# K and q turned on VectorE instead of TensorE, for nine of twelve chunks of a fused attention and MLP kernel

## Chip, cores and metric

One NeuronCore of a Trainium2 chip runs the whole program. The metric is the device time of one execution in microseconds (us); the kernel before takes 1048.77 us, the median of 3 runs (1047.95 to 1049.24).

## Reference

Three layers follow each other. The first is a linear attention with a delta rule: for each of 4 x 8 batch-heads, a 48 x 48 state is read by the query and updated by the key, over 768 positions. The other two are MLPs on 3072 tokens (384 to 2048 to 384), with different activations.

```python
k_n = k / (np.linalg.norm(k, axis=-1, keepdims=True) + 1e-06)
for t in range(S):
    y[:, :, t] = einsum('bhd,bhde->bhe', q[:, :, t], state)
    v_old = einsum('bhde,bhd->bhe', state, kt)
    state = state + bt * einsum('bhd,bhe->bhde', kt, vt - v_old)
# then, on x = y as 3072 tokens x 384:
h = x @ w_in;  x = where(h >= 1, h, where(h <= -1, 0, (h + 1) ** 2 / 4)) @ w_out
h = x @ w_in2; out = (h * clip(h + 3, 0, 6) / 6) @ w_out2
```

## The kernel before

**Attention by chunks.** The 768 positions are cut into 12 chunks (0 to 11) of 64. The 32 batch-heads are 16 units of two heads; a unit's two heads lie in the two halves of the partitions. For a chunk, `front` loads K in natural layout (`KN`), forms norms, brings K and q into transposed layout (`KTT` and `QQ`, head dimension on the partitions, both inside the tile `KQ`; two sets, for even and odd chunks), multiplies them (`products`), and inverts a triangular matrix (`inverse`, most of it as a row of GpSimd steps, L630 and L635, from the transposed matrix that VectorE writes at L688). `chain` then applies the state, forms the update and the output; the output is put into `XB`, 16 rows of each head by a detour over `YS` and a DMA.

**K and q before the change.** For each half `hb` of the batch-heads, `load_tok` (L434) loads K and q with positions on the partitions, two DMAs each of 96 KB in pieces of 192 bytes, into one of two staging buffers `ST`; `transposes` (L516) turns them by four TensorE transposes of 128 columns (L523) into one PSUM bank, and one copy of 112 x 512 out of it follows, on ScalarE or VectorE (L385 or L387); for K a further copy of 112 x 128 repeats a part of it shifted. A chunk has so four groups of four transposes, eight DMAs and four evacuations, and two of the small copies.

**MLP.** Layer 1 runs over seven blocks of tokens: chunk 0, chunk 1, then pairs of chunks. A block goes through 16 slices `f` of the hidden dimension: nine matmuls into a PSUM bank (`H`), an elementwise path (ScalarE L976 and L977, VectorE L978, a copy by L385 into `GH`, VectorE L374 into `GL`), and nine matmuls from `GH` and `GL` (`O`). `O` of a slice is issued after `H` of the next. A finished block leaves by six DMAs (`X<-XB`, L1028). Layer 2 runs over six blocks in the same manner; its weights are loaded into `KQ` once attention has finished with it.

**What sets the order.** The program is a list of operations with dependences (by keys), planned durations and priorities. `Plan.emit` simulates the engines with these durations and takes, per engine, the operation that can start earliest, then the one of lowest priority number; the instructions are issued in that fixed order, so each engine, and the DMA queue of SyncE (SP), works in order. The MLP's elementwise operations have priority 0, those of chunk c about c less 0.2 to 3, and MLP matmuls 50, so attention on TensorE is placed among MLP matmuls, which fill the rest. A change of one operation can change the order of all that comes after it.

Of the kernel before, what the change touches and what calls it, by code (L numbers as in the profile page):

```python
# [23 lines left out]
PR = dict(slots=2, fast=(0,), slate=0, mk=0, hm=0.0, kv=-2.522, tok=-1.749, norm=-2.601, tr=-1.803, prod=-3.087, pm=-0.932, inv=-2.162,  # L24
          sv=0.06, w=-1.449, chain=-0.205, y=-0.76, wl=-0.036, wls=0.003, mp=0, lv=-1.0, first=3.58, bias=83.342, fill=3000,
          tpool=tuple(range(1, 12)), hc=2, halves=1, biasa=652.767, b16=tuple(range(0, 4)), hyst=4058, fgap=150, me=500,
          c3=('act', 'dve', 'pool'), back=1500, dh=0, margin=738.749, umargin=300, urg=('inv', 's'), sw=(217, 95), ad=('act', 'dve'),
          dp=('dve', 'pool'), dg=('dve',), dw=('dve', 'pool'), pq=190)


class Bank:
# [246 lines left out]
def fused_kernel(  # L278
# [15 lines left out]
    nc = tc.nc  # L294
    B, H, S, D = q.shape
    NP = H // 2
    U = B * NP
    CH = 64
# [6 lines left out]
    pool = ctx.enter_context(tc.tile_pool(name="sb", bufs=1, side="left"))  # L305
# [3 lines left out]
    def sb(name, shape, dt=F32):  # L309
        return pool.tile(shape, dt, name=name)  # L310
# [18 lines left out]
    KTT = [KQ[:, i * NK * 160:(i + 1) * NK * 160].rearrange("p (k x) -> p k x", k=NK) for i in range(2)]  # L329
    QP = KQ[:, 2 * NK * 160:].rearrange("p (n u s) -> p n u s", n=4, u=U)  # L330
    QQ = [QP[:, i] for i in range(2)]
# [1 line left out]
    GG = sb("G", [128, 2, U, CH])  # L333
    KN = [sb(f"KN{i}", [128, U, D]) for i in range(2)]
    NST = 2
    ST = [sb(f"ST{i}", [128, NP, 128]) for i in range(NST)]
    X = sb("X", [128, U, CH])
    DL = sb("DL", [128, 32, 32])
    TL = sb("TL", [128, 16, 32])
# [16 lines left out]
    P = Plan()  # L356

    def pri(c, name):
        return c + PR[name] - (PR["first"] if c == 0 else 0)
# [17 lines left out]
    def cpalt(engs, n, out, in_, ps, scale=1.0, **kw):  # L377

        alts = {}
        for e in engs:  # L380
            if e == "pool":
                alts[e] = (190 + 1.1 * n, lambda: nc.gpsimd.tensor_copy(val(out), val(in_)))
            elif e == "act":
                alts[e] = (62 + 0.845 * n if ps else 110 + 0.835 * n,
                           lambda: nc.scalar.activation(out=val(out), in_=val(in_), func=AF.Copy, scale=scale))  # L385
            elif scale == 1.0:
                alts[e] = (62 + 1.05 * n if ps else 67 + 0.53 * n, lambda: nc.vector.tensor_copy(val(out), val(in_)))  # L387
            else:
                alts[e] = (62 + 1.05 * n if ps else 67 + 0.53 * n,
                           lambda: nc.vector.tensor_scalar(out=val(out), in0=val(in_), scalar1=scale, scalar2=None, op0=ALU.mult))  # L390
        return P.op(None, 0, None, alts=alts, port=() if ps else ("dve", "pool"), **kw)
# [31 lines left out]
    extra = [gw[:, 512 * i:512 * i + 512] for i in range(4)]  # L423
    ST += [x.rearrange("p (a x) -> p a x", a=NP) for x in extra]
    for i in range(NST):
        P.op("pool", 470, lambda i=i: nc.gpsimd.memset(ST[i], 0.0), w=[("st", i)])

# [6 lines left out]
    def load_tok(c, hb, src):  # L434
        P.tag = f"tok c{c} h{hb}"
        if c < 2:
            i = (0 if hb == 0 else 2 + 2 * c) + stage[0] % 2
        else:
            i = stage[0] % NST
        stage[0] += 1  # L440
        for b in range(2):
            ap = src[2 * b + hb, :, c * CH:(c + 1) * CH, :].rearrange("h s d -> s h d")
            dst = ST[i][64 * b:64 * b + 64].rearrange("p a (e x) -> p (a e) x", e=2)[:, :, 0:D]
            P.dma(lambda ap=ap, dst=dst: nc.sync.dma_start(out=dst, in_=ap), CH * H, CH * DM * 4,  # L444
                  w=[("st", i, b)], r=[("st", i)], prio=pri(c, "tok") - (0.01 if c == 0 and hb == 0 else 0.0), bulk=c > 0)
        return i

    def nat(src, c, dl):
        return src.rearrange("b (p e) s d -> e s (b p) d", e=2)[dl, c * CH:(c + 1) * CH]
# [26 lines left out]
    def norms(c):  # L476
        P.tag = f"norm c{c}"
        st = c % 2
        pr = pri(c, "norm")
        xk = [("x", hb, g) for hb in range(2) for g in range(2)]  # L480
        sq = X.rearrange("p a b -> p (a b)")[:, 0:U * D].rearrange("p (u d) -> p u d", d=D)
        ttalt(DP, U * D, sq, KN[st], KN[st], ALU.mult,
             r=[("kn", st, 0), ("kn", st, 1)], w=xk, prio=pr)
        s = lambda i: SM[:, i, :]
        W = nc.vector
        P.op("dve", 860, lambda: W.tensor_reduce(out=s(0), in_=sq, axis=mybir.AxisListType.X, op=ALU.add),
             r=xk, w=["sm0"], prio=pr)
        P.op("dve", 82, lambda: W.tensor_scalar_max(s(1), s(0), 1e-30), r=["sm0"], w=["sm1"], prio=pr, port=("dve",))
        P.op("act", 200, lambda: nc.scalar.activation(out=s(2), in_=s(1), func=AF.Sqrt), r=["sm1"], w=["sm2"], prio=pr)
        P.op("dve", 170, lambda: W.reciprocal(out=s(3), in_=s(2)), r=["sm2"], w=["sm3"], prio=pr)  # L490
        P.op("dve", 82, lambda: W.tensor_tensor(out=s(4), in0=s(1), in1=s(3), op=ALU.mult), r=["sm1", "sm3"], w=["sm4"], prio=pr, port=("dve",))
        P.op("dve", 82, lambda: W.tensor_tensor(out=s(5), in0=s(2), in1=s(4), op=ALU.add), r=["sm2", "sm4"], w=["sm5"], prio=pr, port=("dve",))
        P.op("dve", 82, lambda: W.tensor_scalar(out=NRM[st], in0=s(5), scalar1=0.5, scalar2=1e-6, op0=ALU.mult, op1=ALU.add),
             r=["sm5"], w=[("nrm", st)], prio=pr, port=("dve",))
        P.op("dve", 170, lambda: W.reciprocal(out=s(6), in_=NRM[st]), r=[("nrm", st)], w=["sm6"], prio=pr)
        P.op("dve", 82, lambda: W.tensor_tensor(out=s(7), in0=s(6), in1=s(6), op=ALU.mult), r=["sm6"], w=["sm7"], prio=pr, port=("dve",))
        P.op("dve", 82, lambda: W.tensor_tensor(out=D2[st], in0=s(7), in1=BT[:, c, :], op=ALU.mult), r=["sm7", "bt"], w=[("d2", st)], prio=pr, port=("dve",))
        for b in range(4):
            cpalt(PR["c3"], 2 * NK, NT[st][32 * b:32 * b + 32], ND[st][96 - 32 * b:128 - 32 * b, :, NK:U], False,
                  r=[("nrm", st), ("d2", st)], w=[("nt", st, b)], prio=pr, q=qd(96 - 32 * b, None, 32 * b))  # L500
# [15 lines left out]
    def transposes(c, hb, i, is_k):  # L516
        P.tag = f"tr c{c} h{hb} k{is_k}"
        st = c % 2
        bk = Bank()
        pr = pri(c, "tr")  # L520
        def pe():
            for p in range(NP):
                nc.tensor.transpose(bk.tile[0:112, p * 128:(p + 1) * 128], ST[i][:, p, 0:112], IDN)  # L523
        if is_k:
            P.op("pe", 400, pe, load=0.85, r=[("st", i, 0), ("st", i, 1), "idn"], w=[bk], pre=[("kt", st, hb)], alloc=bk, prio=pr)
            ks = slice(hb * NP, (hb + 1) * NP)
            cpalt(AD, 512, KTT[st][0:112, ks, 0:128], lambda: bk.tile[0:112].rearrange("p (a x) -> p a x", a=NP), True, q=(None, 0, 0),
                r=[bk], w=[("kt", st, hb)], pre=[("kr", st, hb)], uses=[bk], prio=pr)
            cpalt(PR["c3"], 128, KTT[st][0:112, ks, 128:160], KTT[st][0:112, ks, 64:96], False,
                  r=[("kt", st, hb)], w=[("kr", st, hb)], prio=pr, q=(0, None, 0))  # L530
        else:
            P.op("pe", 400, pe, load=0.85, r=[("st", i, 0), ("st", i, 1), "idn"], w=[bk], pre=[("qt", st, hb)], alloc=bk, prio=pr)
            o = QQ[st][0:112].rearrange("p (b h a) s -> p h a b s", b=2, h=2)[:, hb]
            cpalt(AD, 512, o, lambda: bk.tile[0:112].rearrange("p (a b s) -> p a b s", a=NP, b=2), True, q=(None, 0, 0),
                r=[bk], w=[("qt", st, hb)], uses=[bk], prio=pr)
# [530 lines left out]
    def front(c):  # L1066
        load_kv(c)
        norms(c)
        for hb in range(2):
            ik = load_tok(c, hb, k)  # L1070
            iq = load_tok(c, hb, q)
            transposes(c, hb, ik, True)
            transposes(c, hb, iq, False)
            products(c, hb)
        xcopies(c)
        if c < 2:
            zero_g(c)
        load_v(c)
        inverse(c)
        scale_v(c)  # L1080
# [3 lines left out]
    for sg in range(2):  # L1084
        src = beta.rearrange("b (p e) s -> e (b p) s", e=2)[sg].rearrange("u (c s) -> u c s", c=NCH)
# [11 lines left out]
    for i in range(4):  # L1097
        zero(ST[2 + i], [("st", 2 + i)], 470)

# [24 lines left out]
    for f in range(NF):  # L1124
        if f == NFA:
            P.op("none", 0, open_wlb, w=[("raw", i) for i in range(NF - NFA)] + [("wlb", True)])
        i = f % (NF - NFA) if f < NFA else NF - NFA
# [25 lines left out]
    for blk, cs in enumerate(blocks):  # L1153
# [6 lines left out]
        n = B * CH * len(cs)  # L1160
# [16 lines left out]
    for i, cs in enumerate(blocks2):  # L1177
        xi = xi2(i)
        xkeys = [("x2b", xi, j, hl) for j in range(KT) for hl in range(2)]
        for f in range(NF):  # L1180
# [9 lines left out]
            a = seq[-2]  # L1190
# [8 lines left out]
    a = seq[-1]  # L1199
# [49 lines left out]
```

## Time and profile before

| quantity | value |
|---|---|
| runs | 1048.77 us median, 1047.95 to 1049.24 |
| the profiled execution | 1050.48 us, of which the span is 1048.7 us |
| mean granted TensorE clock | 0.984 |
| TensorE (PE) busy | 1000.0 us, 95% of the span |
| VectorE (DVE) busy | 597.7 us, 57% |
| ScalarE (ACT) busy | 558.5 us, 53% |
| GpSimd (POOL) busy | 274.6 us, 26%, all of it in layer 1 |

The span is the time between the first and the last instruction on the core. PEld is the weight load of TensorE, which overlaps the matmul before it. PE spans are modelled and overlap at their ends. An engine that is not the bottleneck may idle at no cost, so shares of busy time say little until they are read by stretch.

### The profile page before, as it was taken

How to read it: one execution, taken by the hardware profiler on the slowest of the kernel's cores; microseconds unless marked ns; L12 is line 12 of the kernel's file. 1: busy time of each engine (PE TensorE's matmuls, PEld its weight loads, DVE VectorE, ACT ScalarE, POOL GpSimd, SP SyncE). 2: the span in 40 equal slices, each digit the busy share in tenths (PEclk: the TensorE clock that was granted, in tenths of full speed). 3: DMA queues.
4: the chain of work that ended last, by engine and by line, in shares of the span. 5: the costliest groups of instructions: out<-in, count | busy, mean ns of one | idle time of the engine just before them, and what ended most of it. 6: DMA issues, size and time to landing. Idle time of an engine off the chain costs nothing.

```text
span 1048.7 us, 28665 instructions
## 1 busy us (share of the span) xinstructions
PE 1000.0 (95%) x12085; PEld 856.2 (82%) x12085; DVE 597.7 (57%) x1170; ACT 558.5 (53%) x1155; POOL 274.6 (26%) x668
## 2 busy tenths in 40 slices
PE   6777898899999999999999999999999999999998
PEld 4666888887778787788878788999999999999997
DVE  4878777767677676676545798333333333333333
ACT  5789666574675666656456898223332233322322
POOL 2151413548677485555800000000000000000000
PEclk9878999999999999999999999999999999999999
DMA  6972414223124132220322662201020020200000
GB/s 138 258 173 64 108 34 94 46 48 73 32 49 103 37 62 49 69 56 2 78 83 85 209 198 86 81 29 63 1 91 1 1 91 1 91 1 1 31 1 30
DMA packets 174673, 71.85 MB, mean 69 GB/s; under 512 B 121168, under 2 KB 170448, under 8 KB 174544
## 3 DMA queue, kind: packets, MB, share of 16 engines
q1 hardware_dynamic: 174544, 70.02, 26.2%
q8 instruction: 94, 1.54, 0.6%
q14 instruction: 35, 0.29, 0.1%
HBM read 53.68 MB, written 14.16 MB: 65 GB/s over the span
## 4 chain that ended last, share of the span: by engine, by line
PE 79%; ACT 5%; DMA 5%; DVE 4%; POOL 3%; issue 2%; SPq 1%; DVEq 0%; ACTq 0%; POOLq 0%
PE bank L416 77%; DMA RAWL<-in_moe_w_out_dram 1%; PE bank L523 1%; POOL TMP L630 1%; POOL TL L635 1%; DMA RAWL<-in_moe_w_in_dram 1%; DMA ST<-in_k_dram 1%; DVE GF L978 1%; ACT TBS L919 1%; ACT G L385 1%; SPq L444 1%; ACT GF L976 0%; SPq L898 0%; ACT TBS L385 0%; DMA RAWR<-in_moe_w_out_dram 0%
## 5 line engine op out<-in xcount | busy, mean ns | idle before, releaser
L416 PE MATMUL bank<-XB,WLA 128*128 128x512 f32 (+1 forms) x1404 | 337.8, 383 | 9.6 <-DVE GF L978 5.6
L416 PEld LDWEIGHTS bank<-XB,WLA 128*128 128x128 f32 x1404 | 251.4, 192 | 57.1 <-DVE GF L978 8.7
L374 DVE TENSOR_TENSOR GL<-GF,GH 128x512 fp32r<-128x512 f32 (+1 forms) x208 | 137.5, 663 | 97.5 <-PE bank L416 63.6
L385 ACT ACTIVATE GH<-GF 128x512 fp32r<-128x512 f32 (+1 forms) x206 | 122.7, 597 | 118.3 <-DVE GF L982 69.3
L982 DVE SCALAR_TENSOR_TENSOR GF<-GF,bank 128x512 f32<-128x512 f32 x96 | 66.0, 688 | 192.3 <-ACT GF L981 192.2
L981 ACT ACTIVATE GF<-bank 128x512 f32<-128x512 f32 x96 | 57.4, 598 | 203.1 <-PE bank L416 202.3
L630 POOL TENSOR_TENSOR TMP<-TL,DL 128x126 f32<-128x126 f32 (+25 forms) x293 | 117.3, 400 | 76.2 <-DVE DL L688 40.8
L635 POOL TENSOR_TENSOR TL<-TL,TMP 128x126 f32<-128x126 f32 (+25 forms) x293 | 121.0, 413 | 22.8
L416 PE MATMUL bank<-GH,WLA 128*128 128x512 f32 (+1 forms) x504 | 121.0, 372 | 0.3 <-DVE XB L1021 0.3
L416 PE MATMUL bank<-XB,WLB 128*128 128x512 f32 (+1 forms) x468 | 111.2, 378 | 3.1 <-issue 1.9
L416 PE MATMUL bank<-WLA,GH 128*128 128x384 f32 x576 | 113.2, 338 | 0.0
L416 PEld LDWEIGHTS bank<-WLA,GH 128*128 128x128 f32 x576 | 103.7, 188 | 6.3
L978 DVE SCALAR_TENSOR_TENSOR GF<-bank,GF 128x512 f32<-128x512 f32 (+1 forms) x112 | 68.4, 611 | 58.7 <-ACT GF L977 45.5
L416 PEld LDWEIGHTS bank<-GH,WLA 128*128 128x128 f32 x504 | 86.7, 193 | 15.5 <-DVE XB L1021 0.7
L416 PEld LDWEIGHTS bank<-XB,WLB 128*128 128x128 f32 x468 | 82.9, 188 | 18.3 <-issue 2.0
L976 ACT ACTIVATE GF<-bank 128x512 f32<-128x512 f32 (+1 forms) x112 | 59.8, 534 | 69.2 <-PE bank L416 61.6
L416 PE MATMUL bank<-GL,WLA 128*128 128x512 f32 (+1 forms) x252 | 66.4, 371 | 1.3 <-issue 1.3
L977 ACT ACTIVATE GF<-GF 128x512 f32<-128x512 f32 (+1 forms) x112 | 63.5, 567 | 2.3
L416 PE MATMUL bank<-WLA,GL 128*128 128x384 f32 x288 | 61.5, 334 | 0.0
L416 PEld LDWEIGHTS bank<-WLA,GL 128*128 128x128 f32 x288 | 51.0, 188 | 0.0
L416 PEld LDWEIGHTS bank<-GL,WLA 128*128 128x128 f32 x252 | 43.3, 190 | 8.6 <-issue 1.5
L416 PE MATMUL bank<-GH,WLB 128*128 128x512 f32 (+1 forms) x168 | 38.6, 364 | 0.1
(147 smaller groups left out, 1199.4 us busy)
## 6 DMA issues: line engine op xcount, KB each, us to landing
XB<-X SPq DMA_DIRECT2D x36, 256.0 KB, 4.5
X<-XB SPq DMA_DIRECT2D x30, 256.0 KB, 2.5
KQ<-in_moe_w_in_dram SPq DMA_DIRECT2D x16, 384.0 KB, 4.6
KQ<-in_moe_w_out_dram SPq DMA_DIRECT2D x16, 384.0 KB
KN<-in_k_dram SPq DMA_DIRECT2D x24, 192.0 KB, 3.6
RAWL<-in_moe_w_out_dram SPq DMA_DIRECT2D x12, 384.0 KB, 4.7
out_dram<-E SPq DMA_DIRECT2D x24, 192.0 KB, 1.9
ST<-in_k_dram SPq DMA_DIRECT2D x44, 96.0 KB, 2.8
```

What stands on the lines that cost most here:

```text
L374: alts[e] = (d, lambda e=e: ENG[e].tensor_tensor(out=val(out), in0=val(in0), in1=val(in1), op=op))
L385: lambda: nc.scalar.activation(out=val(out), in_=val(in_), func=AF.Copy, scale=scale))
L416: nc.tensor.matmul(o, l, r, start=start, stop=stop, skip_group_check=skip)
L444: P.dma(lambda ap=ap, dst=dst: nc.sync.dma_start(out=dst, in_=ap), CH * H, CH * DM * 4, w=[("st", i, b)], r=[("st", i)], prio=pri(c, "tok" ...
L523: nc.tensor.transpose(bk.tile[0:112, p * 128:(p + 1) * 128], ST[i][:, p, 0:112], IDN)
L630: P.op(te, d, lambda t=t, s=s, r0=r0, a0=a0, a1=a1, m=m: ve.tensor_tensor(out=t[:, a0:a1], in0=TL[:, r0 + a0:r0 + a1, s:s + 1].to_broadcas ...
L635: P.op(te, d, lambda t=t, s=s, r0=r0, a0=a0, a1=a1: ve.tensor_tensor(out=TL[:, r0 + a0:r0 + a1, 0:s], in0=TL[:, r0 + a0:r0 + a1, 0:s], in1 ...
L976: P.op("act", da, lambda: nc.scalar.activation(out=gf, in_=ps, func=AF.Relu, scale=0.5, bias=0.5), r=hkeys(hb, hv), w=gk, prio=MP)
L977: P.op("act", da + 48, lambda: nc.scalar.activation(out=gf, in_=gf, func=AF.Square), w=gk, r=gk, prio=MP)
L978: P.op("dve", 1.06 * n + 60, lambda: nc.vector.scalar_tensor_tensor(out=gf, in0=ps, scalar=1.0, in1=gf, op0=ALU.max, op1=ALU.min), r=hkeys ...
L981: P.op("act", da, lambda: nc.scalar.activation(out=gf, in_=ps, func=AF.Relu, scale=1.0 / 6.0, bias=0.5), r=hkeys(hb, hv), w=gk, prio=MP)
L982: P.op("dve", 1.06 * n + 60, lambda: nc.vector.scalar_tensor_tensor(out=gf, in0=gf, scalar=1.0, in1=ps, op0=ALU.min, op1=ALU.mult), r=hkey ...
```

## The change

From chunk 3 on (`ct=3`), `front` calls `block_transposes` in place of `load_tok` and `transposes`. The two staging buffers become one tile, seen as `STB` with 1024 elements per partition: 16 units, two halves of 32 positions, 32 elements. Eight DMAs bring a chunk's K (then its q) with 32 positions on 32 partitions, the head dimension cut into 32 and 16: four of them move 512 pieces of 128 bytes, four 512 pieces of 64 bytes. One VectorE instruction then transposes all 32 x 32 blocks of the 128 x 1024 tile straight into `KTT` or `QQ`. The shifted copy is made once for the chunk, over 256 columns. K and q use the same staging tile, so q's DMAs follow the transpose of K and the next chunk's K follows that of q.

```diff
-          dp=('dve', 'pool'), dg=('dve',), dw=('dve', 'pool'), pq=190)
+          dp=('dve', 'pool'), ct=3, dg=('dve',), dw=('dve', 'pool'), pq=190)
...
-    ST = [sb(f"ST{i}", [128, NP, 128]) for i in range(NST)]
+    ST2 = sb("ST", [128, NST, NP, 128])
+    ST = [ST2[:, i] for i in range(NST)]
+    STB = ST2.rearrange("p n a x -> p (n a x)").rearrange("p (u t d) -> p u t d", u=U, t=2)
...
+    def load_blocks(c, src, nm):
+        P.tag = f"tok c{c} {nm}"
+        for dl in range(2):
+            for f in range(2):
+                n = 32 if f == 0 else D - 32
+                p0 = 64 * dl + 32 * f
+                for th in range(2):
+                    ap = src.rearrange("b (p e) s d -> e s (b p) d", e=2)[dl, c * CH + 32 * th:c * CH + 32 * th + 32, :, 32 * f:32 * f + n]
+                    dst = STB[p0:p0 + 32, :, th, 0:n]
+                    P.dma(lambda ap=ap, dst=dst: nc.sync.dma_start(out=dst, in_=ap), 32 * U, 32 * U * 4 * n,
+                          w=[("stb", dl, f, th)], pre=[("st", i, b) for i in range(2) for b in range(2)], prio=pri(c, "tok"), bulk=True)
+
+    def block_transposes(c):
+        st = c % 2
+        sk = [("stb", dl, f, th) for dl in range(2) for f in range(2) for th in range(2)]
+        for nm, src in (("k", k), ("q", q)):
+            load_blocks(c, src, nm)
+            P.tag = f"tr c{c} {nm}"
+            i = STB.rearrange("p (g k) t d -> p g k (t d)", g=2)
+            if nm == "k":
+                o = KTT[st][:, :, 0:128].rearrange("p k (g x) -> p g k x", g=2)
+                P.op("dve", 1180, lambda o=o, i=i: nc.vector.transpose(out=o, in_=i), r=sk, w=[("kt", st, 0), ("kt", st, 1)],
+                     pre=[("kr", st, 0), ("kr", st, 1)], prio=pri(c, "tr"))
+                cpalt(PR["c3"], 256, KTT[st][0:112, :, 128:160], KTT[st][0:112, :, 64:96], False,
+                      r=[("kt", st, 0), ("kt", st, 1)], w=[("kr", st, 0), ("kr", st, 1)], prio=pri(c, "tr"), q=(0, None, 0))
+            else:
+                o = QQ[st].rearrange("p (g k) s -> p g k s", g=2)
+                P.op("dve", 1180, lambda o=o, i=i: nc.vector.transpose(out=o, in_=i), r=sk, w=[("qt", st, 0), ("qt", st, 1)], prio=pri(c, "tr"))
...
+        if c >= PR["ct"]:
+            block_transposes(c)
         for hb in range(2):
-            ik = load_tok(c, hb, k)
...
+            if c < PR["ct"]:
+                ik = load_tok(c, hb, k)
...
             products(c, hb)
```

## Rows read from the trace of the kernel before

**Rows 1.** The chain that ended last, shares of the span by engine.

```profile
PE 79%; ACT 5%; DMA 5%; DVE 4%; POOL 3%; issue 2%; SPq 1%; DVEq 0%; ACTq 0%; POOLq 0%
```

**Rows 2.** Busy time by stretch: stretch, length, engines, clock, DMA share, GB/s.

```profile
85.00:200.00 115.00, 98.28 (x2730) 89.17 (x2721) 88.22 (x213) 78.58 (x195) 35.47 (x97) 0.96 0.34 72
200.00:480.00 280.00, 276.68 (x4783) 223.33 (x4772) 196.85 (x377) 176.72 (x387) 182.66 (x430) 1.00 0.27 56
555.00:660.00 105.00, 103.92 (x464) 85.94 (x463) 78.92 (x159) 82.21 (x163) 0.00 (x0) 1.00 0.49 154
```

**Rows 3.** The same, of the transposes at L523 alone (PE, PEld).

```profile
85.00:200.00 115.00, 6.42 (x40) 4.54 (x40) 0.96 0.34 72
200.00:480.00 280.00, 15.82 (x104) 11.81 (x104) 1.00 0.27 56
```

**Rows 4.** Timeline of PEld: start, duration, engine, line, operation, count.

```profile
206.07 0.45 PEld L523 LDWEIGHTS bank<-IDN,ST 128*112 128x112 f32 x4
206.49 0.42 PEld L416 LDWEIGHTS bank<-GL,WLA 128*128 128x128 f32 x3
```

**Rows 5.** L523, durations in ns: least, median, greatest.

```profile
L523 PE MATMUL bank<-IDN,ST x176: 270/273/447, 8.6 to 470.2; 128*112 128x128 f32 x176
```

**Rows 6.** Groups by shape, ScalarE, 85 to 480 us: count, busy us, mean ns.

```profile
L385 ACT ACTIVATE KQ<-bank 112x512 f32<-112x512 f32 x35 | 20.8, 594 | 10.9 <-PE bank L523 10.3
L385 ACT ACTIVATE KQ<-KQ 112x128 f32<-112x128 f32 x16 | 5.0, 310 | 0.4
```

**Rows 7.** Groups by shape, whole span: VectorE's block transposes.

```profile
L688 DVE STREAM_TRANSPOSE DL<-X 128x1024 f32<-128x1024 f32 x8 | 16.2, 2025 | 2.9 <-PE bank L416 1.5 <-ACT GF L976 1.3
L696 DVE STREAM_TRANSPOSE DL<-TL 128x512 f32<-128x512 f32 x8 | 9.0, 1128 | 0.9 <-POOL TL L635 0.9
L697 DVE STREAM_TRANSPOSE NH<-DL 128x512 f32<-128x512 f32 x12 | 8.4, 703 | 0.2
```

**Rows 8.** Waits of PE from 200 to 555 us: total us, times, longest.

```profile
PE bank L416 <- DVE GF L978: 1.6, 4, 0.6
PE bank L416 <- issue: 0.7, 1, 0.7
```

**Rows 9.** L444 from 200 to 480 us: DMA issue in ns, landing in us.

```profile
L444 SPq DMA_DIRECT2D ST<-in_q_dram x26: 595/596/1108, 202.9 to 465.3; - x26
DMA to landing us min/median/max: 2.5/2.5/2.8
```

**Rows 10.** DMA issues, whole span: count, KB each, median us to landing.

```profile
ST<-in_k_dram SPq DMA_DIRECT2D x44, 96.0 KB, 2.8
E<-in_v_dram SPq DMA_DIRECT2D x48, 48.0 KB, 2.4
XB<-YS SPq DMA_DIRECT2D x66, 32.0 KB, 2.0
```

**Rows 11.** Waits of the SP queue from 200 to 500 us.

```profile
SPq L444 <- PE bank L523: 54.0, 16, 8.5
```

**Rows 12.** Timeline of VectorE: L688 of four chunks, from first to last.

```profile
190.22 2.00 DVE L688 STREAM_TRANSPOSE DL<-X 128x1024 f32<-128x1024 f32 x1
...
234.70 2.04 DVE L688 STREAM_TRANSPOSE DL<-X 128x1024 f32<-128x1024 f32 x1 [0.60 <-PE bank L416]
...
274.74 2.02 DVE L688 STREAM_TRANSPOSE DL<-X 128x1024 f32<-128x1024 f32 x1
...
493.88 2.04 DVE L688 STREAM_TRANSPOSE DL<-X 128x1024 f32<-128x1024 f32 x1 [1.32 <-ACT GF L976]
```

**Rows 13.** Timeline of the SP queue: outputs into XB, finished blocks out.

```profile
203.69 4.39 SPq L867 DMA_DIRECT2D XB<-YS  x6
...
226.94 10.66 SPq L1028 DMA_DIRECT2D X<-XB  x6
...
551.04 3.86 SPq L867 DMA_DIRECT2D XB<-YS  x6
...
578.21 10.93 SPq L1028 DMA_DIRECT2D X<-XB  x6
```

More of the change, by code (lines that the diff above doesn't have):

```diff
@@ L1068, in front @@
         norms(c)
+        if c >= PR["ct"]:
+            block_transposes(c)
         for hb in range(2):
-            ik = load_tok(c, hb, k)
-            iq = load_tok(c, hb, q)
-            transposes(c, hb, ik, True)
-            transposes(c, hb, iq, False)
+            if c < PR["ct"]:
+                ik = load_tok(c, hb, k)
+                iq = load_tok(c, hb, q)
+                transposes(c, hb, ik, True)
+                transposes(c, hb, iq, False)
             products(c, hb)
```

## The prediction, made before the changed kernel ran

> **What bounds the kernel now.** I read the chain of waits first: TensorE holds 79% of it and no other engine more than 5% [rows 1]. A share over the whole span hides the stage that is changed, so the busy time by stretch comes next [rows 2]. The transposes that go are 40 between 85 and 200 us and 104 between 200 and 480 us [rows 3]; 144 is just 9 chunks of 16, so these two stretches hold all of them. From 200 to 480 us PE is busy 276.68 of 280 us at a granted clock of 1.00: it waits 3.3 us in all, and what is taken off PE there is taken off the time, as long as other work keeps it fed. From 85 to 200 us it is busy 98.28 of 115 us (85%): part of what is saved there will only lengthen a wait. VectorE is 70% busy in the second stretch (196.85 of 280), ScalarE 63%, and the DMA engines 27%.
>
> **What goes.** The reader should not take a transpose at its duration. Each lasts 273 ns [rows 5], but they overlap: four start loading at 206.07 and the MLP's next weight load starts at 206.49 [rows 4], so a group of four holds TensorE for 0.42 us. There are 36 groups, 15.1 us in all. The 26 groups in the saturated stretch give 26 x 0.42 = 10.9 us. The 10 groups before 200 us are worth between nothing (if all of it turns into waiting) and 4.2 us; I take the busy share of that stretch, 0.85 x 4.2 = 3.6 us, since the same share of PE's time there is work. With each group goes its evacuation, nearly all on ScalarE: 35 of 594 ns [rows 6], and 18 small copies of 310 ns become 9 of 256 columns. That takes 36 x 0.594 = 21.4 us off ScalarE, which was not the bound; I cost it at nothing, as PE already hides it, and at nothing too the PSUM banks it sets free. At the most these give back PE's wait in the saturated stretch, 3.3 us.
>
> **By the Trainium skill.** The row says 273 ns for one transpose and 0.105 us from one to the next [rows 4, 5]. The Trainium skill, "TensorE: Matmul & The Clock Gate", Part 4, gives about 275 ns for a 128 x 128 transpose in a kernel. The trace agrees with that duration, but whoever multiplies it gets 144 x 0.275 = 39.6 us, where the pitch gives 15.1 us.
>
> **What comes: VectorE.** 18 block transposes of 128 x 1024. None with this pattern is in the trace. L697 turns 128 x 512 out of and into compact rows in 703 ns, L696 with a scattered output in 1128 ns, L688 128 x 1024 out of a scattered input in 2025 ns [rows 7]. The new ones read the tile in order and write runs of 64 elements, so they are nearest to L697: twice that, 1.40 us; the ends are 0.70 us (the larger size free) and 2.03 us (L688). 18 x 1.40 = 25.2 us on VectorE. With 13 of them in the stretch from 200 to 480 us its load there goes from 70% to 77% (18.2 us more), and it stays off the bound. What matters is who stands behind them. VectorE works in order; the MLP's L978 and L374 stand in its queue, and `O` of that slice waits for them on PE. The plan prefers them (priority 0), but a transpose that has started can't be stopped. The nearest rows are the 2.02 us transposes at L688, of which seven fall between 200 and 555 us: there PE waited 1.6 us in all for L978 [rows 8]. If all of that came from those seven it is 0.23 us for each; scaled to 1.40 us, 0.16 us, and 18 x 0.16 = 2.9 us. The ends: nothing (the order `H`, `O` of the slice before, covers it), or the whole of each, 25.2 us. I take 2.9 us, by the row.
>
> **What comes: DMA and the SP queue.** 16 DMAs for a chunk in place of 8. The issue of one takes 0.60 us on SP [rows 9], so 8 x 0.60 = 4.8 us more of SP's time in a chunk, 43 us in all. Landing goes with the number of pieces more than with bytes: 512 pieces of 192 bytes 2.8 us, 256 pieces 2.4 us, 128 pieces 2.0 us [rows 10]. The new ones have 512 smaller pieces; I take 2.8 us, with 2.0 and 5.6 us (double) as ends. A tensor then needs 8 x 0.60 + 2.8 + 1.4 = 9.0 us from its first issue to the end of its transpose, and since q follows K in the same tile, 18 us for a chunk (24 us at the double landing). That fits in a chunk's period: L688 comes from 190.22 to 493.88 in seven steps, 43.4 us each [rows 12]. While q's DMAs wait for K's transpose, what stands behind them in the SP queue waits too: the outputs from `YS`, the v loads, the finished blocks. Before, SP waited in the same way for the PE transposes, 54 us in 16 waits [rows 11], so the wait changes its owner rather than appears. Its cover is the lead of attention over the MLP: chunk 3 is shipped at 203.69 and its block can start when the one before ships at 226.94, chunk 11 at 551.04 against 578.21 [rows 13], 23 and 27 us. I cost all of this at nothing; with the lead gone, each us of lateness would be a us of time. For the first of these chunks K's load now needs both staging buffers free, which the same lead covers.
>
> **The Trainium skill against it.** The rows of DMAs show that pieces of 192 bytes land within 2.8 us [rows 10]. The Trainium skill, "DMA: Bandwidth & Descriptors" (the table at its head), asks for at least 512 bytes in a piece and says that smaller writes become read-modify-write; 64-byte pieces are far below that. No run here shows 64 bytes into these tiles; by the rule the new loads would be late, which is the fourth rival.
>
> **The sum.** -10.9 - 3.6 + 2.9 = -11.6 us. Against the profiled execution of 1050.48 us (span 1048.7 and 1.8 around it) that is 1038.9 us. The median of the runs is 1.7 us below the profiled one; taken from 1048.77 it is 1037.2, and I say 1037 us. Nothing after 555 us changes: the weights of layer 2 are prepared under a PE that is busy 103.92 of 105 us [rows 2], and all of it starts earlier.
>
> **Rivals.**
> 1. *VectorE's queue becomes the bound (slower).* Each transpose stands in front of L978 or L374, and with loads that land later than planned VectorE also waits in order with them behind it. The gain is 10.9 + 3.6 = 14.5 us, so it decides at 14.5 / 18 = 0.81 us of PE stall for each transpose. At 1.40 us each: 1048.77 - 14.5 + 25.2 = 1059 us. For it: 70% load, and ops that can't be broken up. Against it: the 1.6 us for seven longer ones [rows 8].
> 2. *The pace passes to attention's own loop (no change).* L688 comes no closer than 40.0 us (234.70 to 274.74) [rows 12], since one inverse at a time is worked off on GpSimd. The mean period of 43.4 us would fall by 4 x 0.42 = 1.7 us to 41.7; a loop lengthened by two transposes, 42.8 us, would then be the slower one. Against it: 1.1 us in each of 9 chunks eats 10 us of a lead of 27 us [rows 13]. Only if the lead is gone early does the time stay at 1048 to 1049 us.
> 3. *A larger gain.* PE's busy time for the transposes is 22.2 us [rows 3]; if the matmuls behind a group lose its overlapped tail as well, and the stalls stay away, 1048.77 - 22.2 = 1026.5 us. Against it: the MLP's next weight load starts before the group's end [rows 4].
> 4. *Late staging (half the gain).* With landings at 5.6 us or more the products slip and the planned order is kept only with waits on PE; a wait of 0.65 us in each of 9 chunks, half the gain, would be 1037.2 + 5.8 = 1043 us. Against it: the DMA engines are 27% busy [rows 2].
>
> That the change does not do what it says I exclude: `front` is the only caller of both paths.
>
> **How the numbers follow.** The forecast (1031 to 1042 us, from 14.5 + 3.3 us gained to 7 us) has 0.58; rival 1 has 0.18, rivals 2, 3 and 4 have 0.08 each. Faster by over 0.2% (2.1 us, about what a measurement can tell here): 0.58 + 0.08 + 0.08 = 0.74; within 0.2%: 0.08; slower: 0.18. The range is 1028 to 1052 us: it takes in the forecast, rivals 2 and 4, the part of 3 in which not all of the tail is won and the mild part of 1, and leaves out about 0.15.
>
> **What would show it.** PE's busy time from 200 us to the end of attention falls by about 0.42 us a group and its wait there stays under 6 us; block transposes on VectorE near 1.4 us; 1.7 us less between the finished blocks for each chunk. It is wrong if PE's wait for L978 or `GL` rises to some 10 us, if block transposes take 2 us or more, or if the time between two L688 no longer follows the MLP.

## The result, and the profile after

The changed kernel takes 1037.03 us (median of 5 runs, 1031.41 to 1042.25), the kernel before 1048.54 us in the runs beside it: a ratio of 0.9895, 95% interval 0.9855 to 0.9934, so 11.5 us less. The profiled execution takes 1037.03 us with a span of 1035.2 us.

The first look goes to the busy times and the chain, which answer to the table of before and to [rows 1]. First the engines (busy us, share of the span, instructions), then the chain that ended last by engine.

```profile
PE 986.5 (95%) x11941; PEld 841.0 (81%) x11941; DVE 610.3 (59%) x1175; ACT 531.8 (51%) x1102; POOL 286.7 (28%) x689
...
PE 77%; DVE 6%; DMA 5%; ACT 5%; POOL 3%; issue 2%; SPq 2%; DVEq 0%; POOLq 0%; ACTq 0%
```

PE is busy 986.5 us instead of 1000.0. The rest of the span, in which it waits, is 1035.2 - 986.5 = 48.7 us, and before it was 1048.7 - 1000.0 = 48.7 us. The span got shorter by PE's work, 13.5 us, and by nothing else in sum. That the waits are equal does not mean that they are the same ones. The stretches that answer to [rows 2] (stretch, length, PE, PEld, VectorE, ScalarE, GpSimd, granted clock, DMA share, GB/s):

```profile
85.00:200.00 115.00, 101.42 (x2603) 91.17 (x2606) 89.56 (x208) 76.81 (x196) 33.87 (x91) 0.94 0.36 67
200.00:480.00 280.00, 273.62 (x4749) 217.55 (x4738) 210.17 (x388) 157.03 (x338) 200.21 (x470) 1.00 0.32 58
555.00:660.00 105.00, 103.92 (x474) 87.32 (x474) 77.92 (x156) 78.19 (x155) 0.00 (x0) 1.00 0.47 146
```

PE waits 13.6 us between 85 and 200 us (16.7 before) and 6.4 us between 200 and 480 us (3.3 before). VectorE's load in the second stretch went from 70% to 75%, ScalarE's from 63% to 56%, GpSimd's from 65% to 72%. Over the span VectorE is busy only 12.6 us more than before, although its 18 new transposes take 22.4 us: the plan gave other operations to GpSimd, which is busy 12.1 us more. What PE waited for from 200 to 555 us answers to [rows 8] (total us, times, longest); L1009 is the MLP's operation that was L978, L888 writes a chunk's output into `XB`.

```profile
PE bank L418 <- DVE GF L1009: 3.0, 3, 1.8
PE bank L418 <- ACT GH L387: 1.3, 2, 0.8
PE bank L418 <- DVE XB L888: 1.0, 2, 0.6
```

The wait for the MLP's own VectorE operation rose from 1.6 to 3.0 us, and a wait that was not there before appears: of attention's own matmuls, for the VectorE operation that writes a chunk's output. The new block transposes, by shape, beside the one that was taken as the nearest ([rows 7]):

```profile
L477 DVE STREAM_TRANSPOSE KQ<-ST 128x1024 f32<-128x1024 f32 x9 | 11.2, 1244 | 2.7 <-PE bank L418 1.2 <-DMA KN<-in_k_dram 1.1 <-DMA E<-in_v_dram 0.5
L471 DVE STREAM_TRANSPOSE KQ<-ST 128x1024 f32<-128x1024 f32 x9 | 11.2, 1241 | 3.0 <-DMA ST<-in_k_dram 2.9
...
L728 DVE STREAM_TRANSPOSE NH<-DL 128x512 f32<-128x512 f32 x12 | 8.4, 698 | 0.2
```

Each takes 1.24 us, between one and two of the compact 128 x 512 transpose and far from the 2.03 us of the scattered one. The loads, from 200 to 480 us, answer to [rows 9]:

```profile
L459 SPq DMA_DIRECT2D ST<-in_k_dram x48: 317/487/1650, 208.5 to 434.7; - x48
...
DMA to landing us min/median/max: 1.9/2.5/4.1
```

Pieces of 128 and 64 bytes land in 2.5 us, as those of 192 bytes did (the slowest of these DMAs in 4.1 us instead of 2.8), and an issue takes 0.49 us instead of 0.60. Apart, over the whole span (count, KB each, median us to landing; 64 KB are 512 pieces of 128 bytes, 32 KB 512 of 64 bytes, and the 48 KB of v 256 of 192 bytes):

```profile
E<-in_v_dram SPq DMA_DIRECT2D x48, 48.0 KB, 2.6
ST<-in_k_dram SPq DMA_DIRECT2D x36, 64.0 KB, 2.6
...
ST<-in_k_dram SPq DMA_DIRECT2D x36, 32.0 KB, 2.5
```

Last, the SP queue, which answers to [rows 13]: the outputs of chunk 3, 5 and 11 (`XB<-YS`) and the blocks whose end makes room for the MLP on them (`X<-XB`).

```profile
209.43 3.98 SPq L898 DMA_DIRECT2D XB<-YS  x6
...
214.14 1.80 SPq L1059 DMA_DIRECT2D X<-XB  x2
...
296.83 3.95 SPq L898 DMA_DIRECT2D XB<-YS  x6
...
304.26 0.58 SPq L1059 DMA_DIRECT2D X<-XB  x1
...
544.36 3.86 SPq L898 DMA_DIRECT2D XB<-YS  x6
...
564.77 10.92 SPq L1059 DMA_DIRECT2D X<-XB  x6
```

The lead of attention over the MLP, 23 and 27 us for chunks 3 and 11 before, is now 4.7, 7.4 and 20.4 us for chunks 3, 5 and 11. This is the reading that matters most for what follows: in this order the cover that the prediction counted on is nearly used up at the start. The whole gain shows already at 214 us (226.94 before, 12.8 us earlier), although most of the transposes were to come after it: the new order puts MLP work first there and attention later. Chunk 3 comes out 5.7 us later than before and chunk 11 6.7 us earlier. The place of that block is no measure of the gain, for an order alone can move it: in the third order of the kernel before (experiment 5, 1046.68 us) it leaves from 215.29 us on.

```profile
215.29 10.00 SPq L1028 DMA_DIRECT2D X<-XB  x6
```

### The profile page after: what moved, and what is told of

Read it like the earlier page. It is cut to its first block, busy times and chain, and to the rows that moved or that the text cites. A ratio compares the mean times of both kernels' runs of the same rounds, so it can differ in the third digit from the quotient of the medians.

```text
span 1035.2 us, 28435 instructions
## 1 busy us (share of the span) xinstructions
PE 986.5 (95%) x11941; PEld 841.0 (81%) x11941; DVE 610.3 (59%) x1175; ACT 531.8 (51%) x1102; POOL 286.7 (28%) x689
## 4 chain that ended last, share of the span: by engine, by line
PE 77%; DVE 6%; DMA 5%; ACT 5%; POOL 3%; issue 2%; SPq 2%; DVEq 0%; POOLq 0%; ACTq 0%
PE bank L418 77%; DMA RAWL<-in_moe_w_in_dram 2%; DMA KN<-in_k_dram 1%; DMA E<-in_v_dram 1%; POOL TL L666 1%; POOL TMP L661 1%; DVE GF L1009 1%; SPq L446 1%; ACT GF L1007 1%; DMA ST<-in_k_dram 1%; SPq L929 0%; ACT TBS L950 0%; ACT GF L1008 0%; DMA RAWR<-in_moe_w_in_dram 0%; DVE XB L1052 0%
## 5 line engine op out<-in xcount | busy, mean ns | idle before, releaser
L418 PE MATMUL bank<-XB,WLA 128*128 128x512 f32 (+1 forms) x1404 | 334.2, 380 | 14.5 <-DVE GF L1009 9.9
L418 PEld LDWEIGHTS bank<-XB,WLA 128*128 128x128 f32 x1404 | 248.1, 188 | 64.5 <-DVE GF L1009 14.1
L661 POOL TENSOR_TENSOR TMP<-TL,DL 128x126 f32<-128x126 f32 (+25 forms) x293 | 115.2, 393 | 70.4 <-DVE DL L719 33.2
L1009 DVE SCALAR_TENSOR_TENSOR GF<-bank,GF 128x512 f32<-128x512 f32 (+1 forms) x112 | 68.3, 611 | 49.0 <-ACT GF L1008 37.8
L418 PE MATMUL bank<-GH,WLB 128*128 128x512 f32 (+1 forms) x168 | 39.6, 366 | 1.5 <-ACT GH L387 1.5
```

The source lines that it names most:

```text
L418: nc.tensor.matmul(o, l, r, start=start, stop=stop, skip_group_check=skip)
L661: P.op(te, d, lambda t=t, s=s, r0=r0, a0=a0, a1=a1, m=m: ve.tensor_tensor(out=t[:, a0:a1], in0=TL[:, r0 + a0:r0 + a1, s:s + 1].to_broadcas ...
L1009: P.op("dve", 1.06 * n + 60, lambda: nc.vector.scalar_tensor_tensor(out=gf, in0=ps, scalar=1.0, in1=gf, op0=ALU.max, op1=ALU.min), r=hkeys ...
```

## The experiments

Each run stands against runs of the kernel before on the same chip (1048.8, 1047.7 and 1048.2 us in the three groups). One execution of a kernel differs from the next by some us: the kernel before had 1043.81 to 1054.20 us in 22 runs. A difference of 2 us between two of these kernels is no finding.

**1. TensorE's groups put back.** The gain should come back if it is PE's time.

```diff
+    def pe_again(c, key):
+        for n in range(2):
+            bk = Bank()
+            def pe(bk=bk):
+                for p in range(NP):
+                    nc.tensor.transpose(bk.tile[0:112, p * 128:(p + 1) * 128], IDN[:, 0:112], IDN)
+            P.op("pe", 400, pe, load=0.85, r=[(key, c % 2, 0), "idn"], w=[bk], alloc=bk, prio=pri(c, "tr"))
...
+                pe_again(c, "kt")     # after K's block transpose; the same for q
```

> The changed kernel, with the 36 groups of four TensorE transposes put back (of the identity, into a PSUM bank that nobody reads), without their evacuations. Theory (the gain is the TensorE time of the groups): it comes back by 36 x 0.42 = 15 us, 1048 to 1053 us. Rival (the gain comes from ScalarE's 21 us of evacuations that went, or from the new order): it stays at 1041 us or below.

1049.29 us, ratio to before 1.0015 (0.9998 to 1.0031): the gain is gone. The page of its profiled execution, span 1046.9 us:

```profile
PE 998.4 (95%) x12085; PEld 855.2 (82%) x12085; DVE 609.9 (58%) x1173; ACT 537.8 (51%) x1111; POOL 285.2 (27%) x683
```

PE is busy 998.4 us, 11.9 us more than in the changed kernel, at the same granted clock in both early stretches (0.90 up to 85 us and 0.94 up to 200 us in either), and waits 48.5 us. The span differs by 11.7 us. So a group is worth 11.9 / 36 = 0.33 us on average (the medians of the two kernels differ by 12.3 us, 0.34 for each), and that is the gain.

**2. ScalarE's evacuations put back as well.** The run before, with this behind each group:

```diff
+            P.op("act", 62 + 0.845 * 512, lambda bk=bk: nc.scalar.activation(out=bk.tile[0:112], in_=bk.tile[0:112], func=AF.Copy, scale=1.0),
+                 r=[bk], w=[bk], uses=[bk], prio=pri(c, "tr"))
```

> As the run with the TensorE transposes put back, and with 36 evacuations of 112 x 512 put back on ScalarE too (in place in the bank that nobody reads). Theory (ScalarE's relief is worth nothing, PE hides it): within 3 us of that run, 1046 to 1052 us. Rival (the relief of ScalarE and of the PSUM banks is part of the gain): 5 us or more above it, 1054 us or above.

1046.57 us, ratio 0.9994 (0.9970 to 1.0019), no more than without them, with ScalarE busy 554.7 us instead of 537.8. ScalarE's evacuations and the longer hold of the PSUM banks cost nothing that the runs show, as the forecast had it.

**3. Block transposes twice.** Each `P.op("dve", 1180, ...)` stands twice.

```diff
                 P.op("dve", 1180, lambda o=o, i=i: nc.vector.transpose(out=o, in_=i), r=sk, w=[("qt", st, 0), ("qt", st, 1)], prio=pri(c, "tr"))
+                P.op("dve", 1180, lambda o=o, i=i: nc.vector.transpose(out=o, in_=i), r=sk, w=[("qt", st, 0), ("qt", st, 1)], prio=pri(c, "tr"))
```

> Every block transpose of the changed kernel is issued twice, 18 more of 1.24 us on VectorE, nothing else changed. Theory (VectorE stays off the bound; the stall is about 0.2 us for each): 18 x 0.2 = 3.6 us more than the changed kernel, 1037 to 1044 us. Rival (VectorE's queue sets the time): 18 x 1.24 = 22 us more, about 1059 us.

1044.14 us, 7.1 us more than the changed kernel; ratio to before 0.9963 (0.9945 to 0.9980). That is 7.1 / 18 = 0.39 us for each 1.24 us, twice what the theory gave and a third of what the rival gave: just outside the theory's 1037 to 1044, by less than the runs can tell. The load on VectorE did not double with the transposes: it is busy 623.0 us, 12.7 more than in the changed kernel, where 18 transposes are 22 us, since the plan gave other operations to GpSimd (294.9 us instead of 286.7). PE's waits from 200 to 555 us, and its timeline where chunk 3 ends:

```profile
PE bank L418 <- DVE XB L891: 5.3, 4, 1.8
PE bank L418 <- DVE GF L1012: 2.9, 3, 1.6
```

```profile
207.27 0.62 PE L418 MATMUL bank<-GL,WLB 128*128 128x256 f32 x3
...
209.86 1.13 PE L418 MATMUL bank<-E,KQ 48*64 48x48 f32 x60 [1.72 <-DVE XB L891]
212.83 2.56 PE L418 MATMUL bank<-KQ 48*64 48x64 f32 x64 [1.83 <-DVE XB L891]
215.31 1.22 PE L418 MATMUL bank<-XB,WLA 128*128 128x512 f32 x2
```

The MLP's own operation is waited for no longer than in the changed kernel (2.9 us against 3.0). The new wait is of attention's matmuls for L891, which writes a chunk's output, and two thirds of it lie between the last MLP matmuls of one block (207.27) and the first of the next (215.31). VectorE did not hold up the slice of the MLP that ran; attention came late, and its lead was gone (chunk 3's output is issued at 210.2 us, the block before leaves from 208.7 us on). That is a part of the account: PE waits 57.7 us in all instead of 48.7, and 10.9 us instead of 6.4 between 200 and 480 us.

**4. Loads twice.** The DMAs of each staging load are issued twice.

```diff
-        for dl in range(2):
+        for dl in (0, 1, 0, 1):
```

> The changed kernel with the staging loads of K and q issued twice from chunk 3 on: 32 DMAs a chunk in place of 16, 9.6 us more of the SP queue and 8192 more small pieces for each chunk. Theory (the loads are hidden by the lead of attention over the MLP): within 3 us of the changed kernel, 1034 to 1040 us. Rival (late staging costs time): 5 us or more in addition, 1042 us or above.

1045.90 us, ratio to before 0.9987 (0.9968 to 1.0007), 8.9 us more than the changed kernel: the theory fell. Its profile has PE busy 988.2 of 1044.2 us, so 56.0 us of waits against 48.7, in every stretch from 85 to 480 us some more, and a granted clock of 0.84 instead of 0.90 up to 85 us (the run of experiment 2 has 0.84 there too, without doubled loads). The leads are not used up in this profile: chunk 3's output is issued 6.3 us and chunk 5's 5.3 us before the block ahead begins to leave, so by what way the 8.9 us are lost here stays open.

```profile
212.64 3.93 SPq L898 DMA_DIRECT2D XB<-YS  x6
...
218.92 1.26 SPq L1059 DMA_DIRECT2D X<-XB  x2
...
304.68 5.22 SPq L898 DMA_DIRECT2D XB<-YS  x6
...
310.01 0.57 SPq L1059 DMA_DIRECT2D X<-XB  x1
```

To see whether the early stretch alone was to blame, the same from chunk 6 on only:

```diff
+        for dl in ((0, 1, 0, 1) if c >= 6 else (0, 1)):
```

> The changed kernel with the staging loads issued twice from chunk 6 on only (six chunks of nine), where all chunks gave 8.9 us more. Theory (the loads cost only in the stretch before 200 us, where PE waits and its clock falls): within 2 us of the changed kernel, 1035 to 1039 us. Rival (each chunk's loads cost about 1 us wherever it lies): 6/9 of 8.9 us, 1043 us.

1045.37 us, ratio 0.9969 (0.9949 to 0.9989): the theory fell, the place is not the early stretch. The rival's 1043 us, a like cost for each chunk, is exceeded too: six chunks cost 8.3 us, nine 8.9. The runs scatter, from 1038.44 us at a mean granted clock of 0.985 to 1049.04 at 0.972. Here the trace shows a way. The SP queue, from the loads of chunk 6 to the block's end:

```profile
266.21 9.50 SPq L459 DMA_DIRECT2D ST<-in_k_dram  x16
279.29 9.83 SPq L459 DMA_DIRECT2D ST<-in_q_dram  x16
293.99 4.31 SPq L501 DMA_DIRECT2D E<-in_v_dram  x5
298.40 1.31 SPq L486 DMA_DIRECT2D KN<-in_k_dram  x2
...
303.97 2.59 SPq L1059 DMA_DIRECT2D X<-XB  x2
306.64 5.06 SPq L898 DMA_DIRECT2D XB<-YS  x6
```

Chunk 5's output is issued at 306.64, 9.8 us later than in the changed kernel (296.83) and 2.7 us after the block before began to leave, at 303.97: the lead of 7.4 us is used up. PE, from 200 to 555 us and in the timeline behind it:

```profile
PE bank L418 <- DVE XB L888: 6.6, 3, 2.4
PE bank L418 <- DMA XB<-YS: 1.8, 1, 1.8
```

```profile
301.98 0.98 PE L418 MATMUL bank<-GL,WLB 128*128 128x512 f32 x3
...
308.98 2.56 PE L418 MATMUL bank<-KQ 48*64 48x64 f32 x64 [2.43 <-DVE XB L888]
311.92 3.29 PE L418 MATMUL bank<-XB,WLA 128*128 128x512 f32 x6 [0.38 <-ACT KQ L603]
```

From the last MLP matmuls of the one block (301.98) to the first of the next (311.92) PE has only attention's groups, and those wait, by the profile, for L888, which writes a chunk's output: there is no MLP work to fill the time until `XB` is there. The granted clock is 0.95 between 300 and 400 us, where the changed kernel has 1.00. Over the span PE waits 55.4 us, 6.7 more than in the changed kernel, and is busy 991.1 us with the same 11941 instructions, 4.6 more, so waits alone do not make up the loss. Shown is that the output comes late and that PE waits there. What made it late is not taken apart: the SP queue holds 10 us more of issues between 266 and 289 us, but the order changed with it, and chunk 4's output was 4.5 us late already (261.46 against 256.93).

**5. Other orders of the same instructions.** Only a planned duration differs; the list is another one from chunk 3 on.

```diff
-                P.op("dve", 1180, ...)          # the changed kernel, first run
+                P.op("dve", 1244, ...)
...
-            P.op("pe", 400, pe, load=0.85, ...)  # the kernel before, two runs: 420 and 425
+            P.op("pe", 400 if c < 3 else 420, pe, load=0.85, ...)
```

> The changed kernel with the planned duration of the block transposes set to 1244 ns in place of 1180 ns: the same instructions in another order. Theory (the mechanism, not the order, makes the gain): within 3 us of the changed kernel, 1034 to 1040 us. Rival (the gain is the luck of one planned order): anywhere up to 1048 us.

> The kernel before with the planned duration of a transposes group set to 420 ns in place of 400 ns from chunk 3 on: the same instructions in another order. Theory: within 3 us of the kernel before, 1045 to 1052 us. Rival (the order alone is worth as much as the change): below 1042 us.

> The kernel before with the planned duration of a group of transposes set to 425 ns from chunk 3 on: a third order of the same instructions. If the first other order (1060.5 us) was an outlier: 1045 to 1052 us. If the order of the kernel before is a lucky one, and so part of what the change has to beat: 1054 us or above. PE busy 1000 us in either case, the rest is waits.

The changed kernel in another order: 1037.63 us, ratio 0.9904 (0.9880 to 0.9928), the same. The kernel before: 1046.68 us (0.9979, 0.9959 to 0.9999) with 425 and 1060.53 us (ratio 1.0123, 1.0097 to 1.0150) with 420. An order alone can cost 12 us, which neither expectation of that run had. In the profiled execution of the slow one PE was busy as long as before, and the waits make the difference (span 1055.9 us, so 55.8 us of waits):

```profile
PE 1000.1 (95%) x12085; PEld 857.6 (81%) x12085; DVE 600.7 (57%) x1173; ACT 558.1 (53%) x1157; POOL 272.0 (26%) x663
```

So one time of one order proves no mechanism. What carries the verdict is that all five orders with PE's groups in them lie between 1046.6 and 1060.5 us, the two without at 1037.0 and 1037.6 us, and PE's busy time.

**6. Where the change begins.** `ct=3` becomes 7, 5, 2 and 1.

```diff
-          dp=('dve', 'pool'), ct=3, dg=('dve',), dw=('dve', 'pool'), pq=190)
+          dp=('dve', 'pool'), ct=5, dg=('dve',), dw=('dve', 'pool'), pq=190)
```

> The change from chunk 7 on instead of chunk 3, so for five chunks of nine. Theory (each group taken off TensorE is worth the same): busy time of PE 1000.0 - 13.5 x 5/9 = 992.5 us, and 1048.8 - 7.5 = 1041 us, with about 3 us either way for the waits of another order. Rival (the gain is made in the stretch before 230 us, where all of it shows in the finished blocks, by chunks 3 to 5): no gain, 1046 us or above.

> The change from chunk 5 on, so that nothing before about 200 us is changed. Theory (time on PE alone, 28 groups of 36): 1048 - 13.5 x 7/9 = 1037.5 us. If the change costs something in the first 200 us (loads, clock) which is saved here: 1033 to 1036 us. Rival (the gain belongs to the first chunks): 1042 us or above.

> The change from chunk 2 on, four groups more than the changed kernel. If PE's time counts there too: 1.5 us less than the changed kernel, 1035.5 us. If the first 200 us are set by waits and loads (the forecast's discount, taken to its end): no gain or a loss, 1037 to 1042 us.

> The change from chunk 1 on, eight groups more than the changed kernel, all of them in the stretch in which the weights of layer 1 are loaded on the same queue. If PE's time counts: 3 us less, 1034 us. If the additional loads delay the weights there: 1040 us or above.

| first chunk changed | groups off PE | us | ratio to before (95%) |
|---|---|---|---|
| 7 | 20 | 1038.99 | 0.9916 (0.9888 to 0.9944) |
| 5 | 28 | 1033.77 | 0.9857 (0.9835 to 0.9879) |
| 3 | 36 | 1037.03 | 0.9895 (0.9855 to 0.9934) |
| 2 | 40 | 1042.78 | 0.9938 (0.9917 to 0.9960) |
| 1 | 44 | 1046.95 | 0.9986 (0.9968 to 1.0003) |

More groups off PE do not give more from chunk 3 down: with chunks 2 and 1 the gain shrinks, and that a start at 5 gains no less than one at 3 is as far as the intervals go. Each start but the one at 3 was timed in one order only, so an order's luck, up to 12 us in experiment 5, is not taken out of this table. The start at 5 missed its theory (1037.5 us) and lies in the range that was given for a change that costs something in the first 200 us (1033 to 1036). From chunk 5 the lead at chunks 3 and 5 is larger again (16.5 us at chunk 3):

```profile
200.49 4.54 SPq L898 DMA_DIRECT2D XB<-YS  x6
216.99 1.26 SPq L1059 DMA_DIRECT2D X<-XB  x2
```

With chunk 2 in it, the first loss is at 80 us: K's block transpose on VectorE, the shifted copy of K on ScalarE, and PE, which had stood for 6.54 us until then (one timeline, by engine):

```profile
78.00 1.25 DVE L471 STREAM_TRANSPOSE KQ<-ST 128x1024 f32<-128x1024 f32 x1 [0.30 <-issue]
...
79.28 0.42 ACT L387 ACTIVATE KQ<-KQ 112x256 f32<-112x256 f32 x1 [1.00 <-DVE KQ L471]
...
79.83 2.90 PE L418 MATMUL bank<-XB,WLA 128*128 128x256 f32 x12 [6.54 <-ACT KQ L387]
```

In the changed kernel PE's first MLP matmul there starts at 71.27 us. The profile puts the wait down to the copy of K, by the end of the one and the start of the other; the matmul itself does not read that copy, so that this is the cause is the profile's inference and no more. With chunk 1 in it, that first MLP matmul starts at 81.65 us. Until then the plan fills TensorE's idle time with matmuls on the tile `GH` into a bank that nobody reads (fillers), and there are 181 of them instead of 73 (the changed kernel, then the one from chunk 1 on; durations in ns, first and last start; then PE's timeline):

```profile
L418 PE MATMUL bank<-GH x73: 388/389/795, 5.2 to 69.5; 128*128 128x512 f32 x73
```

```profile
L418 PE MATMUL bank<-GH x181: 387/389/795, 5.2 to 79.5; 128*128 128x512 f32 x181
```

```profile
81.65 0.95 PE L418 MATMUL bank<-XB,WLA 128*128 128x256 f32 x6 [0.39 <-DVE E L780]
```

The first MLP matmul comes 8.6 us later with chunk 2 and 10.4 us later with chunk 1, and the kernels are 5.8 and 9.9 us slower than the changed one. That the delay is the loss is likely and not shown. The busy times of PE have to be read with this, from chunk 5 on and from chunk 1 on:

```profile
PE 986.3 (96%) x11973; PEld 844.1 (82%) x11973; DVE 608.5 (59%) x1176; ACT 535.7 (52%) x1108; POOL 286.3 (28%) x685
```

```profile
PE 1002.3 (96%) x12017; PEld 856.1 (82%) x12017; DVE 615.6 (59%) x1175; ACT 530.8 (51%) x1091; POOL 289.9 (28%) x692
```

With 44 groups off, PE is busier than before the change, by the fillers. With 28 groups off it is as busy as with 36, at the same mean clock of 0.984.

The kernel from chunk 5 on is clearly faster than the kernel before, by 1.4%. Against the changed kernel it has the better median by 3.3 us, but the intervals overlap, so that it beats it is likely and not shown. Chunk 7 gave 8.7 us and chunk 5 14.4 us, where 20 and 28 groups at 0.33 us would be 6.6 and 9.2 us: 0.33 us is a mean over the 36 groups and need not be the worth of each. For chunk 7 the clock may have a part in it: its profiled execution had a mean granted clock of 0.992 instead of 0.984, and its four runs go from 1036.16 us at 0.992 to 1040.44 us at 0.983.

## Why the prediction was right, and where it was not

**What bounds it** held. The first view, the chain by engine, and the busy time by stretch led to PE's time as the thing to count, and experiments 1 and 2 show that it is the gain and that ScalarE's is not.

**The gain of PE, 10.9 + 3.6 = 14.5 us,** was right in kind and 22% too large. The run with the groups put back gives 11.9 us, 0.33 us for each on average instead of 0.42. Whether the pitch between two weight loads holds a part of the neighbours' own time the rows don't say. The duration of one transpose, 39.6 us in all, would have been too large by a factor of 3.3. Which of the two terms was too large is not shown. Experiment 6 points at the second: the 28 groups from chunk 5 on bring 14.4 us (12.7 to 17.3 by the interval), so the 10.9 us for the 26 of the saturated stretch were not too much, while the groups of chunks 3 and 4 bring nothing in sum, as far as the intervals and a single order of the kernel from chunk 5 on go. The discount for the stretch before 200 us was then in the right direction and too small.

**The stall of VectorE, 2.9 us,** came out at nothing in sum (48.7 us of waits before and after), with 1.4 us more wait for the MLP's operation. A transpose takes 1.24 us, not 1.40, and VectorE got 12.6 us of work more instead of 25.2, since the plan moved other operations to GpSimd. Rival 1 needed 0.81 us of stall for each; even with twice as many it was 0.39 us, and that by another way than the one it named.

**The loads, costed at nothing behind a lead of 23 to 27 us,** is the step that only just held. It took the lead from the profile of before as if the change left it alone. But the change eats it from both ends: the MLP's blocks come earlier by 12.8 us, and chunk 3, with its loads one after the other, comes 5.7 us later. What was left, 4.7 and 7.4 us, was enough for the kernel as it is. With doubled transposes the lead of chunk 3 was used up, with loads doubled from chunk 6 on that of chunk 5; with all loads doubled 6.3 and 5.3 us stayed and the time rose all the same, so the lead is not the whole account (experiments 3 and 4). Rival 4 had the right place but not its mechanism: the pieces land as fast as before (2.5 us); what costs, where the traces show it, is that a chunk's output comes after the MLP has run out of work. That landing goes with the number of pieces was read from rows in which the bytes fell with the pieces; now 512 pieces of 64 bytes land in 2.5 us and 256 of 192 bytes in 2.6, so the number does not decide either. The Trainium skill, "DMA: Bandwidth & Descriptors" (the table at its head), gives 512 bytes as the least transfer for the full rate, with read-modify-write below it. That rule does not tell these loads apart: 64 and 128 bytes land in the time of 192, and with all three below 512 the step at 512 is not tested here.

**Rival 2, the pace passing to attention's loop,** did not happen. The time between two inverses is 41.9 us, from 194.82 to 488.05 us in seven steps, with 41.7 forecast for attention at the MLP's pace and 42.8 for the longer loop; that it is near 41.7 is chance, for the MLP's own pace was another (see the signs). The two ends (line L719 was L688):

```profile
194.82 2.00 DVE L719 STREAM_TRANSPOSE DL<-X 128x1024 f32<-128x1024 f32 x1
...
488.05 2.04 DVE L719 STREAM_TRANSPOSE DL<-X 128x1024 f32<-128x1024 f32 x1 [0.45 <-PE bank L418]
```

**The signs** that were named: PE's wait from 200 us to the end of attention should stay under 6 us (it is 6.4, a near miss), block transposes near 1.4 us (1.24), and 1.7 us less between the finished blocks for each chunk. The last one failed: the blocks after 214 us take as long as before in sum (the last one begins to leave at 631.91 instead of 645.37, 13.5 us earlier, the first 12.8 us). The shift was there at once because the order moved, and the attention that was put off, late by 5.7 us at chunk 3, was caught up by chunk 11, 6.7 us early. That its missing groups set free the time for it is the likely reading. Of the signs of being wrong, 10 us of wait for the MLP's operation (3.0) and transposes of 2 us did not come. The third, inverses that no longer follow the MLP, did: they are 41.9 us apart, while the MLP took 43.8 us a chunk between 214.14 and 564.77 us, because attention was catching up.

The sum met the time to 0.2 us, 1037.2 against 1037.0. Part of that is luck: the gain 2.6 us too large and the stall 2.9 us too large cancel, and an order by itself can be worth 12 us.

## What to carry to other kernels

Where one engine is saturated, count what an edit takes off it by the pitch of its instructions, and test it by putting that work back without its consumers; the engine's busy time then separates work from waits, as long as the plan adds no fillers and the granted clock is the same. A cover that hides new transfers must be read after the change: an edit that speeds the consumer and delays the producer uses the same lead from both ends, and the next small addition is no longer free. In a kernel whose order comes from a list scheduler, time a second order before one time is believed.

## What the runs showed of the hardware

- VectorE turned 128 x 1024 in 32 x 32 blocks in 1.24 us when the input ran in order and the output in order (q) or in runs of 64 elements (K), and the same size in 2.03 us from a scattered input; 128 x 512 took 0.70 us in order and 1.13 us with a scattered output.
- A DMA of 512 pieces of 64 or 128 bytes landed in 2.5 us like one of 512 pieces of 192 bytes, and its issue took 0.49 us instead of 0.60.
- The granted clock of TensorE was at the lower of its two levels, 1.2 and 2.4 GHz, in parts of the first 130 us in all of these kernels (0.84 to 0.98 of the higher one on average up to 85 us, PE busy some 67% to 85% there), and the share changed from one run of a kernel to the next, with 4 us between the runs at a mean of 0.992 and 0.983 in experiment 6. The order of the instructions is fixed in a kernel, so it doesn't fix the clock. Nor does the mean clock explain every difference: the changed kernel took 1031.41 us in a run at 0.984 and 1042.25 us in one at 0.985.
